# Four-layer attention kernel: the steps of layer A in another order (loads and statistics early, keys alternating with queries, G in halves, P read three tiles ahead)

## The chip, the cores and the metric

The kernel runs on one core of a Trainium2 chip. Five engines work side by side, each through a queue of its own in order: TensorE (PE: matrix products, which read SBUF and write PSUM; its weight loads, PEld, overlap the products), VectorE (DVE), ScalarE (ACT), GpSimd (POOL) and SyncE (SP, which here only issues DMAs). Semaphores make one engine wait for another. The metric is device time in microseconds (us) of the whole program; less is better.

## The reference

Four layers, A B A B, act on x of 2048 tokens by 640 values, each with 32 heads of 20 values and added to its own input. Layer A is linear attention over all tokens:

```
phi = lambda t: where(t > 0, t + 1, exp(t)) + 1e-6
pq, pk = phi(q), phi(k)                       # q, k, v = layernorm(x) @ wqkv
kv  = einsum("bhsd,bhse->bhde", pk, v)
z   = einsum("bhsd->bhd", pk)
num = einsum("bhqd,bhde->bhqe", pq, kv)
den = einsum("bhqd,bhd->bhq", pq, z)[..., None] + 1e-6
x   = x + reshape(num / den) @ wo
```

Layer B is softmax attention within four segments of 512 tokens, joined by a gate with a memory that earlier segments left. The change touches layer A alone.

## The kernel before, in words

**Numbers.** x is fp32. A matrix product takes each operand as a high and a low fp16 part and adds three products (high by high, high by low, low by high), so a product over 640 values, five blocks of 128, is 15 matmuls. Half a tile of tokens (128 tokens by 320 columns) is one such group of 15, in `proj_n` (L340 to 350); the text calls it a *unit*. A tile has two, a segment four tiles.

**Layer A in two passes.** All tokens' keys must be summed before any query can be answered. So the first pass (`a_first`, L451) makes, for each segment: normalized x (`norms`, L423: loads at L301, statistics at L304 to 316, normalized tile at L320), its transposes on PE (`turn`, L290), which ACT and DVE split into the two parts of `xT` (L294, L295), and `xs`, the normalized x split without transposing (L441, L442); then 8 units of keys (L458) and 8 of queries (L473), each followed by phi (`phi_a`, L355: ACT exp L359 and relu L361, POOL min and add L362, DVE addition L363). phi of keys, `pk`, is split by ACT (L464) and DVE (L465) and added to z (L470). phi of queries, P, is stored to DRAM by a DMA from POOL's queue (L476). Then `memory` (L479) multiplies keys with x itself, not with v: G = xsᵀ·pk, ten products of 12 matmuls (L489), five for the first half of the columns and five for the second, added to G by DVE (L496).

**The merge.** After the last segment's G, `merge` (L511) adds z over the partitions by PE (L526), copies it to `zb` (L527) and takes reciprocals (L528), scales G by them and splits it (L538 to L540), multiplies by the weight of v (L553: `kt`, evacuated by DVE and ACT at L558 to L565) and by the output weight (L583, L588: `wm`, L590, L591). `wm` then stands for k, v and the output at once. The last segment's query units are not needed for that and *fill* PE while ACT and DVE work on the steps of the merge.

**The second pass** (`a_second`, L628) reads P back tile by tile (`a_read`, L603: load on SP, POOL multiplies by zb at L608, DVE sums per head at L611 and L612, inverts, and multiplies at L614 into `pqi`), transposes it on PE and multiplies by `wm`. It reads two tiles ahead; `a_head` (L618) reads the first two and transposes the first. The second pass is woven with layer B's projections.

**What sets the order.** Only PE's order is the order in which the program is written; the tile scheduler orders DVE, ACT, POOL and SP by it with some freedom, each of them again in order once set. Steps are Python generators: `chain` runs them one after the other, `weave(main, aux, per)` takes `per` steps of the second after each of the first. The first layer A has nothing else to run beside it; its function `opening` (L951) weaves each segment's first pass with the preparation of seven weights (`w_prep`, L206: loads on SP, absolute maximum on DVE at L216 and L221, a transpose and a product on PE at L224 and L229 with DVE's L226 between, scales L232 to L235, splits by ACT L239 and DVE L240, and a store to DRAM on SP at L245) and with the next segment's `norms`. The second layer A runs beside layer B's attention in its first two segments and alone in the last two.

**Buffers.** Tiles tagged `row` (x, normalized x, pk, P) share ROWS = 10 buffers, phi's results share PQ = 5, and there are eight PSUM banks.

Of the kernel before, what the change touches and what calls it, by code (L numbers as in the profile page):

```python
# [21 lines left out]
P = 128  # L22
# [75 lines left out]
def weave(main, aux, per=1, drain=True):  # L98

    while True:  # L100
        try:
            r = next(main)
        except StopIteration as e:
            if drain:
                for r in aux:
                    yield r or 0.0
            return e.value
        yield r
        if not callable(r):
            for _ in range(per):  # L110
                x = next(aux, None)
                if x:
                    yield x


# [10 lines left out]
class Kernel:  # L126
# [295 lines left out]

    def norms(self, src, s, box, then=None):  # L423

        m = []
        for i in range(NT):
            m.append(self.moments(self.load_x(src, s, i)))
            if i == 0 and then:
                then()
        yield 0.0  # L430
        box.append(self.x_t())
        o = s % 2
        xs = self.sb.tile([P, C, 2, D], F16, tag="wo" if o else "w", name="xs", bufs=2 if o else 3)
        box.append(xs)
        nc = self.nc
        xh = self.normed(*m[0])
        yield 0.0
        for i in range(NT):
            nx = self.normed(*m[i + 1]) if i + 1 < NT else None
            yield from self.turn(xh, box[0], i)  # L440
# [10 lines left out]
    def a_first(self, s, box, w, L, behind=None):  # L451


        nc, sb = self.nc, self.sb
        xT, xs = box
        pk = []

        def keys():  # L458
            for i in range(NT):
                pk.append(sb.tile([P, 2, D], F16, tag="row", name="pk", bufs=ROWS))  # L460
                for n in range(2):
                    c = slice(n * HN, (n + 1) * HN)
                    e = self.phi_a(self.proj_n(xT, w("k"), i, n), self.inv["A", "k"])
                    nc.scalar.activation(pk[i][:, 0, c], e, AF.Copy, scale=self.k_scl)  # L464
                    nc.vector.scalar_tensor_tensor(pk[i][:, 1, c], e, self.k_scl, pk[i][:, 0, c],  # L465
                                                   op0=OP.mult, op1=OP.subtract)
                    if s == 0 and i == 0:
                        nc.vector.tensor_copy(L["z"][:, c], e)
                    else:
                        nc.vector.tensor_tensor(L["z"][:, c], L["z"][:, c], e, op=OP.add)  # L470
                    yield self.COST_N

# [25 lines left out]

        yield from keys()
        if s < NSEG - 1:  # L500
            for i in range(NT):
                yield from queries(i)
            if behind:
# [7 lines left out]
    def merge(self, L, wv, wo, fill):  # L511

# [31 lines left out]
        kt = []  # L544
        for t in range(C):
# [21 lines left out]
            yield 15 * (hi - lo) * COL  # L567
            if t % 2:
                yield from filled(1)
        wm = sb.tile([P, C, 2, D], F16, tag="wo", name="wm", bufs=2)  # L570
        yield from filled(1)
        for u in range(C):
            for n in range(2):
# [19 lines left out]
                yield 6 * HN * COL  # L593
            yield from filled(1)
        L["wm"] = wm
# [22 lines left out]
    def a_head(self, L, s, box):  # L618
# [5 lines left out]
        yield from self.a_read(L, s, 0, box["o"])  # L624
        yield from self.a_read(L, s, 1, box["o"])
        yield from self.turn(box["o"][0], box["oT"][0], 0)

    def a_second(self, src, dst, s, L, box, norm):  # L628
# [322 lines left out]
    def opening(self, src, stage, L, box):  # L951
# [13 lines left out]

        def w(n):
            if n != "v":
                for _ in a(n):
                    pass
            return self.w["A", n]  # L970

# [10 lines left out]
        k = a("k")  # L982
        n = self.norms(src, 0, cur, lambda: next(k))
        for _ in range(6):
# [7 lines left out]
        for s in range(NSEG):  # L992
            nxt = []
            if s == 0:
                aux = chain(a("q"), self.norms(src, 1, nxt), prep(("A", "v"), False))
            elif s == 1:
                aux = chain(prep(("A", "o"), False), self.norms(src, 2, nxt), late(), prep(("B", "v"), False))
            elif s == 2:
                aux = chain(self.norms(src, 3, nxt), prep(("B", "q"), False), prep(("B", "k"), False))
            else:  # L1000
                self.scales("A")
                self.w["A", "v"] = self.fetch(("A", "v"))
                aux = chain(prep(("B", "o"), False), last(), self.a_head(L, 0, box))
            yield from weave(self.a_first(s, cur, w, L), aux, per=2)
            cur = nxt

    def dense(self, layers, stage_ctx):
# [15 lines left out]
        while i < n:  # L1023
# [38 lines left out]
            else:  # L1062
                self.rate = R_MID
                for k in "kq":
                    wA[k] = self.fetch(("A", k))
                w = wA.__getitem__
                L = self.a_begin(i + 2)
                src = xs[i + 2]
                x0, x1, x2, x3 = [], [], [], []
                over = lambda st: lambda: st.get("attended")  # L1070
                yield from weave(fin, self.norms(src, 0, x0))
                yield from weave(self.a_first(0, x0, w, L, over(segs[2])),
                                 chain(when(segs[2], "attended", out[2]), self.norms(src, 1, x1)))
                yield from weave(self.a_first(1, x1, w, L, over(segs[3])),
                                 chain(when(segs[3], "attended", out[3]), self.norms(src, 2, x2)))
                yield from weave(self.a_first(2, x2, w, L), self.norms(src, 3, x3))
                wA["v"] = self.fetch(("A", "v"))
                yield from weave(self.a_first(3, x3, w, L), self.a_head(L, 0, box))
            i += 2
# [62 lines left out]
```

## Time and profile before

| | us |
|---|---|
| median of 3 runs (lowest, highest) | 1990.2 (1985.79, 1992.05) |
| the profiled execution | 1985.85 |
| its span in the trace | 1984.1 |
| PE busy | 1723.9 (87%) |
| DVE busy | 1298.5 (65%) |
| ACT busy | 963.8 (49%) |
| POOL busy | 636.7 (32%) |

The span runs from the first to the last recorded instruction; the profiled execution's own time has 1.75 us around it. Its mean granted TensorE clock is 0.959 of full speed. In the opening, 0 to 45 us hold the first normalized tiles and the preparation of the key weight; keys and queries of segments 0, 1 and 2 lie at 45 to 84 (keys of segment 0 begin earlier), 100 to 162 and 178 to 235 us, their G behind each for 16.3 us; keys of segment 3 at 251, its G at 268, its merge from 291 to 340. The second layer A's segment 2 begins at 1143 us, its last merge ends at 1292.

A row of the waits reads "PE ps L290 <- ACT xh L320: total us, times, longest": PE's instruction at L290, which writes `ps`, waited for ACT's instruction at L320, which writes `xh`. In a row of the timeline the numbers ahead are the start and the time in us, x5 counts the instructions, and the brackets at the end have the idle time before them and what ended it.

### The profile page before, as it was taken

What the parts mean: (1) busy time and instruction counts of PE and PEld (TensorE: products, weight loads), DVE (VectorE), ACT (ScalarE), POOL (GpSimd) and SP (SyncE); (2) the same over time, 40 slices, a digit from 0 to 9 for tenths busy, and PEclk for the clock granted to TensorE, in tenths of its full rate; (3) what the DMA queues carried; (4) which work ended last, traced back from release to release, by engine and by line L of the source; (5) the groups of instructions that cost most, each with busy time, mean ns of one, the idle gap of its engine ahead of it and who ended that gap; (6) DMA issues with size and microseconds to landing.
All of it is one profiled execution on the core that took longest, in us unless ns stands there. A gap on an engine that the chain in (4) does not pass through costs nothing.

```text
span 1984.1 us, 36713 instructions
## 1 busy us (share of the span) xinstructions
PE 1723.9 (87%) x13032; PEld 1056.0 (53%) x13032; DVE 1298.5 (65%) x4135; ACT 963.8 (49%) x1826; POOL 636.7 (32%) x1059
## 2 busy tenths in 40 slices
PE   4867887988898898999889989899889898898998
PEld 3545664655455456445545766565445544544555
DVE  7575656457677767767775454644767776767884
ACT  5453523334654554556555352323465466455553
POOL 3544535102222222324444453510221232222321
PEclk9887998999999999999999999899999999999999
DMA  5333334231222232323220312224123212323332
GB/s 192 131 129 117 126 133 164 90 129 48 71 94 65 88 108 80 103 93 114 68 91 14 107 34 100 107 89 147 56 71 99 94 58 95 105 61 95 127 101 87
DMA packets 107376, 192.55 MB, mean 97 GB/s; under 512 B 14124, under 2 KB 65452, under 8 KB 104504
## 3 DMA queue, kind: packets, MB, share of 16 engines
q1 hardware_dynamic: 93032, 137.44, 21.6%
q0 software_dynamic: 4944, 31.79, 4.4%
q10 hardware_dynamic: 9216, 20.98, 2.8%
q8 instruction: 103, 1.69, 0.4%
q14 instruction: 81, 0.66, 0.1%
HBM read 110.96 MB, written 78.64 MB: 96 GB/s over the span
## 4 chain that ended last, share of the span: by engine, by line
PE 58%; DVE 17%; POOL 9%; issue 8%; ACT 6%; DMA 2%; SPq 0%; POOLq 0%; ACTq 0%; DVEq 0%
PE ps L347 21%; PE ps L333 12%; PE ps L881 8%; DVE junk L824 6%; POOL e L362 5%; PE ps L489 4%; PE ps L854 3%; PE ps L290 3%; ACT pe L858 2%; PE ps L817 2%; PE ps L399 2%; PE ps L712 1%; DVE e L363 1%; POOL xs L442 1%; PE ps L894 1%
## 5 line engine op out<-in xcount | busy, mean ns | idle before, releaser
L824 DVE CUSTOM_DVE_ANT_0 junk<-ps,maskw 128x512 bf16<-128x512 f32 (+3 forms) x1024 | 498.9, 487 | 80.1 <-PE ps L817 27.3
L858 ACT ACTIVATE pe<-ps,lsc 128x512 f32<-128x512 f32 x640 | 394.2, 693 | 168.2 <-PE ps L854 142.2
L865 POOL TENSOR_SCALAR_AFFINE_SELECT pe<-pe 128x256 f32<-128x256 f32 (+1 forms) x640 | 236.7, 378 | 647.8 <-ACT pe L858 639.0
L347 PEld LDWEIGHTS <-xT 128*128 128x128 f16 x2880 | 287.8, 101 | 130.1 <-issue 17.5
L347 PEld LDWEIGHTS <-oT 128*128 128x128 f16 x1920 | 188.5, 99 | 88.0 <-issue 12.2
L362 POOL TENSOR_SCALAR e<-e 128x320 f32<-128x320 f32 x128 | 173.0, 1352 | 167.6 <-ACT e L359 163.1
L881 PE MATMUL ps<-pe,v 128*32 128x512 f32 (+3 forms) x2048 | 176.7, 477 | 11.9 <-POOL pe L865 4.6
L363 DVE TENSOR_TENSOR e<-e,r 128x320 f32<-128x320 f32 x128 | 64.5, 504 | 164.3 <-POOL e L362 163.3
L854 PE MATMUL ps<-qs,ks 62*128 62x384 f16 (+3 forms) x1024 | 130.3, 298 | 30.5 <-DVE mg L824 23.7
L347 PE MATMUL ps<-w_Aq,xT 128*128 128x320 f16 x960 | 147.7, 313 | 1.1 <-DVE mg L824 1.1
L347 PE MATMUL ps<-wm,oT 128*128 128x320 f16 x960 | 148.4, 309 | 0.0
L347 PE MATMUL ps<-w_Ak,xT 128*128 128x320 f16 x960 | 145.7, 311 | 1.3 <-DVE mg L824 0.7
L489 PE MATMUL ps<-pk,xs 128*128 128x320 f16 x960 | 138.3, 303 | 9.8 <-ACT pk L464 7.8
L347 PE MATMUL ps<-w_Bo,oT 128*128 128x320 f16 x960 | 141.2, 299 | 2.2 <-DVE mg L824 1.0
L333 PE MATMUL ps<-xT,w_Bq 128*128 128x512 f16 x600 | 140.3, 379 | 2.2 <-ACT r L372 1.2
L347 PE MATMUL ps<-w_Bv,xT 128*128 128x320 f16 x960 | 139.6, 299 | 2.5 <-DVE mg L824 2.5
L333 PE MATMUL ps<-xT,w_Bk 128*128 128x512 f16 x600 | 138.9, 380 | 0.6 <-DVE mg L824 0.6
L489 PEld LDWEIGHTS <-xs 128*128 128x128 f16 x960 | 94.7, 99 | 51.0 <-issue 13.9
L881 PEld LDWEIGHTS ps<-pe,v 128*32 128x32 f32 x2048 | 72.0, 117 | 89.5 <-issue 70.1
L817 PE MATMUL ps<-ks,qs 60*128 60x512 f16 (+3 forms) x1024 | 111.5, 298 | 8.7 <-DVE mg L824 4.4
L313 POOL TENSOR_TENSOR rs<-rs,mhalf 128x1 f32<-128x1 f32 x64 | 35.4, 553 | 238.2 <-DVE rs L312 237.3
L677 DVE SCALAR_TENSOR_TENSOR nat<-ps,nat 128x512 f16<-128x512 f32 x80 | 55.3, 691 | 85.6 <-ACT nat L676 82.4
(184 smaller groups left out, 2464.4 us busy)
## 6 DMA issues: line engine op xcount, KB each, us to landing
x<-xn ACTq DMA_DIRECT2D x48, 320.0 KB
qs<-qd SPq DMA_DIRECT2D x128, 120.0 KB
ks<-kd SPq DMA_DIRECT2D x128, 120.0 KB
xo<-x SPq DMA_DIRECT2D x48, 320.0 KB
pqd<-e POOLq DMA_DIRECT2D x64, 160.0 KB, 2.2
pqi<-pqd SPq DMA_DIRECT2D x32, 320.0 KB
qd<-nat SPq DMA_DIRECT2D x40, 256.0 KB
kd<-nat SPq DMA_DIRECT2D x40, 256.0 KB
```

The source lines that it names most:

```text
L290: nc.tensor.transpose(pt[:, (c - c0) * P:(c - c0 + 1) * P], src[:, c * P:(c + 1) * P], self.ident)
L333: nc.tensor.matmul(p, w[:, c, a, t * P:(t + 1) * P], xT[:, c, b, :], start=k == 0, stop=k == 3 * C - 1)
L347: nc.tensor.matmul(p, xT[:, c, a, i * P:(i + 1) * P], w[:, c, b, n * HN:(n + 1) * HN], start=k == 0, stop=k == 3 * C - 1)
L362: nc.gpsimd.tensor_scalar(e, e, 1.0, 1e-6, op0=OP.min, op1=OP.add)
L363: nc.vector.tensor_tensor(e, e, r, op=OP.add)
L489: nc.tensor.matmul(p, xs[:, i, a, c * P:(c + 1) * P], pk[i][:, b, n * HN:(n + 1) * HN], start=k == 0, stop=k == 3 * NT - 1)
L817: nc.tensor.matmul(bs[par][:, a:a + n], qs[r, p, i * P:(i + 1) * P], ks[r, p, :n], start=True, stop=True)
L824: nc.vector.tensor_tensor_reduce(junk[:, :n], bs[par][:, a:a + n], self.maskw[:, SEG - n:], 1.0, NEG, OP.add, OP.max, G["mg"][:, par, p, i ...
L854: nc.tensor.matmul(b[:, a:a + n], ks[r, p, j * P:(j + 1) * P], qs[r, p, j * P:], start=True, stop=True)
L858: nc.scalar.activation(e, b, AF.Exp, scale=self.lsc)
L865: nc.gpsimd.affine_select(d, d, pattern=pat, compare_op=OP.is_ge, fill=0.0, base=0, channel_multiplier=-1)
L881: nc.tensor.matmul(G["pv"][32 * h4:32 * h4 + 32, j * P:], v[j][:, h * E1:h * E1 + 32], G.pop((p, par, j)), start=j == 0, stop=j == 2, skip ...
```

## The change

`norms` is split: `moments_of` loads four tiles and takes their statistics, `norms` does the rest. In the opening, moments come ahead of a weight's preparation in each segment's auxiliary steps, and in segments 1 to 3 one auxiliary step is taken at a time instead of two. In the second layer A `norms` waits for eight more steps in the last but one segment (`pause`).

Keys and queries alternate, a tile of each in turn, if the query weight is there when the first pass of the segment starts. In the opening's first segment it isn't: there all keys go first, as before. The weight is there by the time the test is made again, and `queries(NT - 1)` is then issued once more: the last tile of queries is computed and stored twice, with the same values.

In the last segment two query tiles alternate with the keys, and two are left to fill. The z product comes ahead of G; G is made inside the merge, five products, then scaling and splitting of the first half beneath the other five; the two units of one query tile go in after the second `kt` tile, of the other two units one ahead of the products of `wm` and one behind them. `ones_column` comes later. `a_head` reads three tiles and waits for `wm`; `a_second` reads three ahead.

```diff
-    def norms(self, src, s, box, then=None):
+    def moments_of(self, src, s, box, then=None):
         m = []
         for i in range(NT):
             m.append(self.moments(self.load_x(src, s, i)))
             if i == 0 and then:
                 then()
+        box.append(m)
         yield 0.0
+    def norms(self, s, box):
+        nc, m = self.nc, box[0]
         box.append(self.x_t())
...
-        yield from keys()
-        if s < NSEG - 1:
+        if w("q", False) is None:
+            for i in range(NT):
+                yield from keys(i)
             for i in range(NT):
                 yield from queries(i)
+        else:
+            for i in range(NT - 1):
+                yield from keys(i)
+                if s < NSEG - 1 or i < 2:
+                    yield from queries(i)
+            yield from keys(NT - 1)
+        if s < NSEG - 1:
+            if w("q", False) is not None:
+                yield from queries(NT - 1)
             if behind:
                 yield behind
             yield from memory()
         else:
             wo = self.fetch_as(("A", "o"), ("A", "k"))
-            yield from memory()
-            yield from self.merge(L, w("v"), wo, chain(*(queries(i) for i in range(NT))))
+            yield from self.merge(L, w("v"), wo, memory(), chain(queries(2), queries(3)))
...
         L["zb"] = zb
         gs = []
         for n in range(2):
+            for _ in range(C):
+                yield next(memory)
             t = self.x_t()
             gs.append(t)
             for c in range(C):
...
-            yield from filled(2)
-        for v in L["v"]:
-            self.ones_column(v)
+        for _ in memory:
+            pass
...
-            if t % 2:
-                yield from filled(1)
+            if t == 1:
+                yield from filled(2)
+        for v in L["v"]:
+            self.ones_column(v)
         wm = sb.tile([P, C, 2, D], F16, tag="wo", name="wm", bufs=2)
         yield from filled(1)
         for u in range(C):
...
-            yield from filled(1)
         L["wm"] = wm
         yield from filled(8)
...
         yield from self.a_read(L, s, 0, box["o"])
         yield from self.a_read(L, s, 1, box["o"])
+        yield from self.a_read(L, s, 2, box["o"])
+        while L["wm"] is None:
+            yield 0.0
         yield from self.turn(box["o"][0], box["oT"][0], 0)
...
-            if i + 2 < NT:
-                yield from self.a_read(L, s, i + 2, o)
+            if i + 3 < NT:
+                yield from self.a_read(L, s, i + 3, o)
...
-                aux = chain(a("q"), self.norms(src, 1, nxt), prep(("A", "v"), False))
+                aux = chain(a("q"), self.moments_of(src, 1, nxt), prep(("A", "v"), False), self.norms(1, nxt))
             elif s == 1:
-                aux = chain(prep(("A", "o"), False), self.norms(src, 2, nxt), late(), prep(("B", "v"), False))
+                aux = chain(self.moments_of(src, 2, nxt), prep(("A", "o"), False), self.norms(2, nxt), late(),
+                            prep(("B", "v"), False))
             elif s == 2:
-                aux = chain(self.norms(src, 3, nxt), prep(("B", "q"), False), prep(("B", "k"), False))
+                aux = chain(self.moments_of(src, 3, nxt), prep(("B", "q"), False), self.norms(3, nxt),
+                            prep(("B", "k"), False))
...
-            yield from weave(self.a_first(s, cur, w, L), aux, per=2)
+            yield from weave(self.a_first(s, cur, w, L), aux, per=2 if s == 0 else 1)
...
-                yield from weave(self.a_first(2, x2, w, L), self.norms(src, 3, x3))
+                yield from weave(self.a_first(2, x[2], w, L), chain(moments(3), pause(8), norms(3)))
```

Where that moves instructions, shown at three places. On SP, the opening around the loads of segment 2's x (`in_A_x`; `stage` receives a weight, `wd_Ao` is the store of a prepared one). Before:

```order
L214 DMA stage<-in_B_wv 128x640 x5
L301 DMA x<-in_A_x 128x640
L245 DMA wd_Ao<-split 128x6400
L301 DMA x<-in_A_x 128x640 x3
L214 DMA stage<-in_B_wq 128x640 x5
```

The same place after:

```order
L219 DMA stage<-in_B_wv 128x640 x5
L306 DMA x<-in_A_x 128x640 x4
L250 DMA wd_Ao<-split 128x6400
L219 DMA stage<-in_B_wq 128x640 x5
L250 DMA wd_Bv<-split 128x6400
```

All four loads stand ahead of the store now; the next weight's loads and its store follow.

On PE, the product of z with a matrix of ones (`square`) in the first layer's last segment. Before:

```order
L489 LDWEIGHTS xs
L489 MATMUL ps<-pk,xs 128x320
L526 MATMUL ps<-z,square 128x320 x2
L347 LDWEIGHTS xT
L347 MATMUL ps<-w_Aq,xT 128x320
```

The same place after:

```order
L352 LDWEIGHTS xT
L352 MATMUL ps<-w_Ak,xT 128x320
L544 MATMUL ps<-z,square 128x320 x2
L497 LDWEIGHTS xs
L497 MATMUL ps<-pk,xs 128x320
```

It stood between G (L489) and the query units that fill; it stands between the last key unit (L352) and G (L497) now.

On POOL, the second segment of the opening, from its first steps of phi (`e`) to the first store of P (`pqd_1`); `rs` belongs to the statistics of the next x tiles, `xs` to their split. Before:

```order
L362 TENSOR_SCALAR e<-e 128x320 x7
L313 TENSOR_TENSOR rs<-rs,mhalf 128x1
L442 TENSOR_TENSOR xs<-xh,xs 128x640
L313 TENSOR_TENSOR rs<-rs,mhalf 128x1 x2
L442 TENSOR_TENSOR xs<-xh,xs 128x640
L313 TENSOR_TENSOR rs<-rs,mhalf 128x1
L362 TENSOR_SCALAR e<-e 128x320
L442 TENSOR_TENSOR xs<-xh,xs 128x640
L362 TENSOR_SCALAR e<-e 128x320
L476 DMA pqd_1_97<-e 128x320
```

The same place after:

```order
L367 TENSOR_SCALAR e<-e 128x320 x3
L318 TENSOR_TENSOR rs<-rs,mhalf 128x1 x2
L367 TENSOR_SCALAR e<-e 128x320
L318 TENSOR_TENSOR rs<-rs,mhalf 128x1
L484 DMA pqd_1_97<-e 128x320
L318 TENSOR_TENSOR rs<-rs,mhalf 128x1
L484 DMA pqd_1_97<-e 128x320
L367 TENSOR_SCALAR e<-e 128x320 x3
L484 DMA pqd_1_97<-e 128x320
```

The statistics stand some four steps of phi earlier, the splits `xs` behind them, and stores of P come among the keys' steps.

More of the change, by code (lines that the diff above doesn't have):

```diff
@@ L113, in weave, with pause @@
                     yield x
+def pause(n):
+    for _ in range(n):
+        yield 0.0
 def when(state, key, gen):
@@ L454, in a_first, with keys @@
         nc, sb = self.nc, self.sb
-        xT, xs = box
+        _, xT, xs = box
         pk = []
[L458 to L471, printed above, removed]
+        def keys(i):
+            pk.append(sb.tile([P, 2, D], F16, tag="row", name="pk", bufs=ROWS))
+            for n in range(2):
+                c = slice(n * HN, (n + 1) * HN)
+                e = self.phi_a(self.proj_n(xT, w("k"), i, n), self.inv["A", "k"])
+                nc.scalar.activation(pk[i][:, 0, c], e, AF.Copy, scale=self.k_scl)
+                nc.vector.scalar_tensor_tensor(pk[i][:, 1, c], e, self.k_scl, pk[i][:, 0, c],
+                                               op0=OP.mult, op1=OP.subtract)
+                if s == 0 and i == 0:
+                    nc.vector.tensor_copy(L["z"][:, c], e)
+                else:
+                    nc.vector.tensor_tensor(L["z"][:, c], L["z"][:, c], e, op=OP.add)
+                yield self.COST_N
         def queries(i):
@@ L964, in a, with w @@
             return preps[n]
-        def w(n):
-            if n != "v":
+        def w(n, now=True):
+            if now and n != "v":
                 for _ in a(n):
                     pass
-            return self.w["A", n]
+            return self.w.get(("A", n)) if now or ("A", n) in self.wd else None
         def late():
@@ L982, in opening @@
         k = a("k")
-        n = self.norms(src, 0, cur, lambda: next(k))
+        n = chain(self.moments_of(src, 0, cur, lambda: next(k)), self.norms(0, cur))
         for _ in range(6):
```

25 lines of the change are left out of this document (14 added, 11 removed).

## The prediction

> **What bounds the kernel now.** I read the shares first, then PE's waits in the stretches that the change touches, then a table of those stretches, then single rows. PE works for most of the span:
>
> ```profile
> PE 1723.9 (87%) x13032; PEld 1056.0 (53%) x13032; DVE 1298.5 (65%) x4135; ACT 963.8 (49%) x1826; POOL 636.7 (32%) x1059
> ```
>
> So a gain must come out of PE's idle time. The views of PE's waits say where that is: for 0 to 341 us (the first layer A up to its second pass), for 1140 to 1293 (the second layer A from segment 2 to its second pass), and, last line, for 341 to 930 (in 1293 to 1984 this row is the same). Columns: total us, times, longest us.
>
> ```profile
> PE ps L290 <- ACT xh L320: 42.9, 8, 11.3
> PE ps L229 <- DVE wm L226: 21.2, 6, 7.3
> PE ps L290 <- DVE rca L612: 8.7, 1, 8.7
> PE ps L224 <- DVE wm L221: 4.9, 1, 4.9
> PE ps L489 <- ACT pk L464: 3.1, 2, 2.6
> PE ps L588 <- ACT kt L564: 3.1, 1, 3.1
> ...
> PE ps L290 <- ACT xh L320: 8.3, 3, 5.7
> PE ps L290 <- DVE pqi L614: 5.3, 1, 5.3
> PE ps L489 <- ACT pk L464: 4.6, 1, 4.6
> PE ps L588 <- ACT kt L564: 3.1, 1, 3.1
> ...
> PE ps L290 <- DVE pqi L614: 7.4, 2, 4.1
> ```
>
> A transpose (L290) waits for a normalized tile or for a P tile, a weight's tiny product (L229) for its statistics. Each stands in PE's fixed order, so everything behind it stands too. The table by stage (stretch, length, busy PE, PEld, DVE, ACT, POOL, granted clock, DMA share, GB/s) has the keys and queries of segments 0, 1 and 2 of the opening, G of segment 3, its merge, the start of the second pass; then, of the second layer A, the keys and queries of segment 2, G of segment 3, its merge:
>
> ```profile
> 45.00:84.10 39.10, 25.14 (x159) 17.65 (x160) 26.63 (x65) 22.53 (x43) 23.21 (x22) 0.83 0.35 131
> 100.40:162.20 61.80, 40.39 (x268) 28.23 (x266) 42.29 (x94) 33.70 (x64) 31.15 (x29) 0.83 0.31 111
> 178.50:235.00 56.50, 42.61 (x269) 29.37 (x268) 28.95 (x75) 31.96 (x63) 30.17 (x27) 0.85 0.18 63
> 268.10:291.30 23.20, 18.64 (x123) 12.48 (x121) 12.69 (x24) 4.83 (x11) 4.90 (x5) 0.93 0.55 199
> 291.30:340.50 49.20, 36.75 (x299) 23.00 (x298) 32.12 (x67) 17.45 (x42) 27.13 (x30) 0.86 0.36 130
> 340.50:364.70 24.20, 20.90 (x146) 15.39 (x146) 14.42 (x37) 6.37 (x13) 4.34 (x6) 0.93 0.56 186
> 1142.90:1188.50 45.60, 37.30 (x262) 26.57 (x260) 26.68 (x60) 27.21 (x57) 26.88 (x24) 0.93 0.07 25
> 1221.10:1244.00 22.90, 18.10 (x123) 12.29 (x121) 9.53 (x20) 4.38 (x10) 4.43 (x4) 0.93 0.20 73
> 1244.00:1292.10 48.10, 39.09 (x300) 24.73 (x298) 31.30 (x68) 16.97 (x42) 27.45 (x30) 0.86 0.30 110
> ```
>
> Length less PE's busy time is idle time: 14.0 + 21.4 + 13.9 + 4.6 + 12.5 + 3.3 = 69.7 us in the first six stretches, 8.3 + 4.8 + 9.0 = 22.1 in the last three. Busy time is stretched too, since the clock is 0.83 to 0.93 there. Prices at full clock come from PE's timeline:
>
> ```profile
> 53.18 1.33 PE L290 MATMUL ps<-ident,xh 128*128 128x128 f32 x5 [8.23 <-ACT xh L320]
> 61.16 0.71 PE L290 MATMUL ps<-ident,xh 128*128 128x128 f32 x5
> 61.70 2.20 PE L347 MATMUL ps<-w_Aq,xT 128*128 128x320 f16 x15
> 84.09 16.46 PE L489 MATMUL ps<-pk,xs 128*128 128x320 f16 x120
> ```
>
> A matmul of 320 columns costs 16.46/120 = 137 ns, a unit of 15 (half a tile of keys or queries) 2.06, five transposes 61.70 − 61.16 = 0.54.
>
> **The change, part by part.** Line numbers are those of before.
>
> *Segment 1* of the opening now loads and measures segment 2's x tiles before any weight, and takes auxiliary steps one at a time, not two, so that more of them lie beside G. Before, three of the four loads stood on SP behind a store that waited for a weight's splits until 121.95, 21.5 us into the segment:
>
> ```profile
> 121.95 0.33 SPq L245 DMA_DIRECT2D wd_Ao<-split  x1
> 122.37 2.63 SPq L301 DMA_DIRECT2D x<-in_A_x  x3
> ```
>
> With that gone, what is late next is DVE. At full clock PE needs 16 units (33.0), 20 transposes (2.2) and 8 small matmuls (0.8); with 2.5 of waits and 1 for the clock that is 39.5 against 61.8, a gain of 22. But DVE was busy for 42.29 of those 61.8 us, and unless part of that slips into G it is the longer of the two: I take 20 (12 to 23).
>
> *Segment 2* gets its x tiles early, and segment 3's loads now stand behind another store, that of w_Bv. PE needs 33.0 + 2.2 + 0.9, 1.5 for the clock, and I add 7 for new waits: w_Bv's splits ahead of key work on ACT and DVE (2.7), the late loads (3), others (1.3). That is 44.6 against 56.5: 12 (9 to 16).
>
> *Segment 0* keeps keys before queries. Its long wait begins at 53.18 − 8.23 = 44.95, and I leave it there: w_Av's statistics now stand on PE ahead of the transposes, and DVE comes to them no earlier than
>
> ```profile
> 52.09 1.53 DVE L216 TENSOR_REDUCE wmx<-stage 128x1 f32<-128x640 f32 x2
> 53.66 0.16 DVE L221 TENSOR_REDUCE wm<-wmx 128x1 f32<-128x5 f32 x1
> ```
>
> By the second test of the weight it is ready, so the last tile of queries is issued twice: 30 matmuls, 4.1 us on PE, and two exponential steps and stores on POOL, hidden behind G. Of the idle 14.0 about 8 stays; the other 6, and about 1 of clock, go: 3 (0 to 5).
>
> *Keys and queries alternating.* POOL's steps for the exponentials followed each other by 76.14 − 73.35 = 2.79 for queries and 111.63 − 108.73 = 2.90 for keys, where PE needs 2.06:
>
> ```profile
> 73.35 1.27 POOL L362 TENSOR_SCALAR e<-e 128x320 f32<-128x320 f32 x1
> 75.45 0.61 POOL L476 DMA_DIRECT2D pqd<-e  x1 [0.82 <-DVE wm L226]
> 76.14 1.27 POOL L362 TENSOR_SCALAR e<-e 128x320 f32<-128x320 f32 x1
> 108.73 1.28 POOL L362 TENSOR_SCALAR e<-e 128x320 f32<-128x320 f32 x1 [4.20 <-ACT e L359]
> 111.63 1.28 POOL L362 TENSOR_SCALAR e<-e 128x320 f32<-128x320 f32 x1 [1.62 <-ACT e L359]
> ```
>
> A key's steps go from ACT to POOL, DVE and back to ACT, one after the other; a query's fill the gaps, and POOL's own work for one of each is 1.28 + 1.27 + 0.61 = 3.16, under PE's 4.12. So I let PE set the pace; that it doesn't is rival B.
>
> *Segment 3 and its merge* take, with keys of 8 × 2.06, 16.5 + 23.2 + 49.2 = 88.9. The merge's PE work less z (1.1, four short matmuls), 8 units and about 2 of slow clock is 36.75 − 1.1 − 16.5 − 2 = 17.2; with the four units that are left to fill it, 25.5. After: 12 units (24.7), 0.8 of small work, z 1.1, a wait, G 16.5, the 25.5, and 1.5 for the clock. The wait is new in size. G waits for the last pk now too, 4.6 in the second layer; but the z product, ahead of G now, waits for the last addition to z, and its copy, reciprocal and scaling of half 0 stand in DVE's queue ahead of the last key unit's own steps. By the group row the reciprocal is 2.12; the other two are put at 0.53 and 0.25, an estimate from the addition's row:
>
> ```profile
> L470 DVE TENSOR_TENSOR z<-z,e 128x320 f32<-128x320 f32 x30 | 15.8, 527 | 0.4
> L528 DVE RECIPROCAL rz<-zb 128x320 f32<-128x320 f32 x2 | 4.2, 2120 | 0.0
> ```
>
> 4.6 + 2.9 is 7.5; w_Bo's preparation shares ACT and DVE here, so I put it at 9 (5 to 12). The sum is 79.1, a gain of 10 (5 to 14). In exchange G's scaling for half 0 lies beneath half 1, P's first tiles are read further ahead (8.7 us of wait) and kt has two fill units behind it.
>
> *The second layer A.* Segment 2 has 33.0 + 2.2 and some 2 of waits left, 37 from 45.6: 8.5 (5 to 9); pause(8) puts its transposes behind their loads. Segment 3 with merge was 16.5 + 22.9 + 48.1 = 87.5; by the same terms, with 7 for the wait and 26 for the merge, 24.7 + 1.1 + 7 + 16.5 + 1 + 26 = 76.3: 11 (7 to 14). Segments 0 and 1 lie beside attention, which fills PE: 0 (−3 to 3).
>
> *P read three tiles ahead* in the second passes: the 7.4 us row, twice, is 14.8, and up to 2.4 of slow clock behind each. A third tile ahead adds two units of cover, 4.1 us, as long as the longest wait. Its row buffer is one of ten, and a wait for one could give some back: 15 (10 to 19.6).
>
> Sum: 20 + 12 + 3 + 10 + 8.5 + 11 + 15 = 79.5. The profiled execution took 1985.85, so 1906.35; the median of the runs shown is 1990.2, 4.35 more: 1910.7, rounded to 1911.
>
> One rule speaks against the alternation. The Trainium skill, page "SBUF — State Buffer", section "SBUF: two separate sides", says that a DVE instruction with two SBUF inputs and a GpSimd instruction that reads SBUF exclude each other, and that the one which starts second is blocked for the whole of the other. Alternation lays more of POOL's steps beside DVE's additions, so by this rule the sum would go the way of rival D. In the trace the mean z addition takes 527 ns (row above), and the longest is
>
> ```profile
> 1162.19 1.36 DVE L470 TENSOR_TENSOR z<-z,e 128x320 f32<-128x320 f32 x1
> ```
>
> so it bears the rule out for single instructions at most, and the sum keeps 0.53.
>
> **The rivals.**
>
> A, the forecast: 1911. Half the widths of the seven ranges and of ±3, taken as independent, make about ±12; its own range is 1896 to 1926. Chance 0.68.
>
> B, the chains set the pace of keys and queries though they alternate: 8 × 2.90 + 8 × 2.79 = 45.5 per segment against 33.0, 12.5 more in each of three (segments 1 and 2 here, segment 2 there), less some 2 that segment 1 already sets aside: 35.5 more, 1946. For it speaks DVE's 42.29 us in segment 1, against it that the two chains leave each other gaps on every engine. Chance 0.18.
>
> C, new waits at their low ends, each term at its high one: 23 + 16 + 5 + 14 + 9 + 14 + 19.6 + 3 = 103.6, so 1887. Chance 0.08.
>
> D, slower: POOL's steps hold each two-input DVE step of these stretches to 1.36, where it takes 0.53: 0.83 more. Three steps per key unit and one per query unit are 32 per segment, 26.6 us; with 28 in a last one, 23.2: 3 × 26.6 + 2 × 23.2 = 126 us. If more than 79.5/126 = 63% of that lies on PE's path, the gain is gone; at 80% it is 101, 21 slower, 2011. The mean of 527 ns speaks against it. Chance 0.04.
>
> E, the waits only move to the next instruction in PE's order: 1990, within 0.3% (6 us, about what a measurement of this kernel can tell from no change). For it: every stretch has several kinds of wait in a row. Chance 0.02.
>
> **How the numbers follow.** 1911 is A's. The range reaches from C's time to B's, 1887 to 1946: half of B, half of C, D and E, together 0.19, lie outside. Faster are A, B and C, 0.94; the same, E, 0.02; slower, D, 0.04.
>
> **What would show it.** In the changed profile, transposes of x should wait nowhere for more than 3 us in segments 1 and 2, but for 6 us or more near 45; the clock should be near 1 in those stretches; query matmuls with w_Aq should count 990; G of segment 3 should have 5 to 12 us of wait ahead of it; the second passes should have no 4 us wait for P. B would show as many waits of under a microsecond for PSUM banks or for pk, D as z additions with a mean above 0.8 us. Segments 1 and 2 at more than 50 us each, or new waits for row buffers in the second passes, would make the forecast wrong.

## The result and the profile after

The changed kernel takes 1916.9 us (median of 4 runs, 1911.5 to 1930.5) beside 1988.0 (4 runs, 1983.9 to 1992.1) for the kernel before: ratio 0.965, 95% interval 0.960 to 0.971. It is 71 us faster; 77 were forecast (1988 to 1911). The profiled execution took 1911.5 and is the fastest of the four; its gain on the profiled one of before is 74.4 us, and the terms below are measured against that.

PE's busy time fell by 20.7 us although it has 30 matmuls more, so part of the gain is clock (a mean of 0.959 of full speed before, 0.970 after); the rest of the 74 is idle time:

```profile
PE 1703.2 (89%) x13062; PEld 1048.7 (55%) x13062; DVE 1290.3 (68%) x4137; ACT 961.8 (50%) x1830; POOL 639.3 (33%) x1063
```

PE's waits in the changed kernel, first for 0 to 300 us, then for 1060 to 1230 (the second layer A's last segments). From 300 us to the end of the first merge at 312.6 PE shows no wait, so the first view stands against that of before for 0 to 341:

```profile
PE ps L295 <- ACT xh L325: 17.2, 4, 7.2
PE ps L544 <- ACT pk L472: 14.9, 2, 10.7
PE ps L295 <- DMA x<-in_A_x: 10.9, 1, 10.9
PE ps L229 <- DVE wm L226: 10.6, 2, 5.9
PE ps L234 <- DVE wm L231: 7.0, 4, 3.1
...
PE ps L544 <- ACT pk L472: 13.3, 2, 9.1
PE ps L295 <- ACT xh L325: 10.7, 2, 7.9
```

The waits for statistics (L229, L234) shrank from 26.1 to 17.6. Those for normalized tiles (L295 on `xh`) are smaller but not gone (11.3 of before's 42.9 us were the kernel's first wait, which has a row of its own here, for the load of x), and a new one stands at the z product (L544), which now precedes G: 14.9 and 13.3 us (the rows name ACT's pk, which ends beside the addition to z on DVE that the product reads). The places, from PE's timeline:

```profile
81.44 16.46 PE L497 MATMUL ps<-pk,xs 128*128 128x320 f16 x120
...
143.28 0.90 PE L295 MATMUL ps<-ident,xh 128*128 128x128 f32 x3 [7.16 <-ACT xh L325]
143.98 4.21 PE L352 MATMUL ps<-w_Aq,xT 128*128 128x320 f16 x15
...
201.39 0.90 PE L295 MATMUL ps<-ident,xh 128*128 128x128 f32 x3 [6.59 <-ACT xh L325]
...
264.86 1.40 PE L544 MATMUL ps<-z,square 128*128 128x320 f32 x2 [10.67 <-ACT pk L472]
270.47 1.41 PE L544 MATMUL ps<-z,square 128*128 128x320 f32 x2 [4.21 <-ACT pk L472]
271.67 17.95 PE L497 MATMUL ps<-pk,xs 128*128 128x320 f16 x120
...
1129.13 0.90 PE L295 MATMUL ps<-ident,xh 128*128 128x128 f32 x3 [7.88 <-ACT xh L325]
```

With the starts of each stretch in PE's timelines of both kernels, the gain lies elsewhere than forecast:

| stretch (its end) | before, us | after, us | gain | forecast |
|---|---|---|---|---|
| up to G of segment 0 | 84.1 | 81.4 | 2.7 | 3 |
| G of segment 0 | 16.3 | 16.3 | 0 | 0 |
| segment 1, with its G | 78.2 | 68.6 | 9.6 | 20 |
| segment 2, with its G | 72.7 | 62.7 | 10.0 | 12 |
| segment 3 and merge, to the first P transpose after it | 89.2 | 83.6 | 5.6 | 10 |
| second passes and layer B, and the second layer A's segments 0 and 1 | 802.4 | 786.0 | 16.4 | 7.5 |
| second layer A, segment 2 with G | 61.9 | 66.6 | −4.7 | 8.5 |
| its segment 3 and merge | 87.3 | 82.0 | 5.2 | 11 |
| the last second pass and layer B | 692.0 | 662.5 | 29.5 | 7.5 |

The first passes where layer A runs alone gave 28 us, not the 64.5 forecast for these six terms; the rest gave 46, not 15.

### The profile page after: what moved, and what is told of

It is laid out like the page before. It is cut to its first block, busy times and chain, and to the rows that moved or that the text cites. A ratio compares the mean times of both kernels' runs of the same rounds, so it can differ in the third digit from the quotient of the medians.

```text
span 1909.8 us, 36713 instructions
## 1 busy us (share of the span) xinstructions
PE 1703.2 (89%) x13062; PEld 1048.7 (55%) x13062; DVE 1290.3 (68%) x4137; ACT 961.8 (50%) x1830; POOL 639.3 (33%) x1063
## 4 chain that ended last, share of the span: by engine, by line
PE 35%; DVE 6%; ACT 3%; POOL 3%; issue 3%; POOLq 0%; ACTq 0%; DVEq 0%
PE ps L352 13%; PE ps L338 6%; PE ps L904 4%; PE ps L497 4%; DVE junk L847 3%; POOL e L367 2%; PE ps L877 2%; PE ps L295 2%; ACT pe L881 1%; PE ps L840 1%; PE ps L735 1%; PE ps L404 1%; PE ps L917 1%; DVE nat L700 1%; ACT nat L699 0%
## 5 line engine op out<-in xcount | busy, mean ns | idle before, releaser
L352 PEld LDWEIGHTS <-xT 128*128 128x128 f16 x2910 | 288.9, 100 | 129.7 <-issue 17.6
L352 PEld LDWEIGHTS <-oT 128*128 128x128 f16 x1920 | 185.4, 98 | 87.5 <-issue 11.8
L904 PE MATMUL ps<-pe,v 128*32 128x512 f32 (+3 forms) x2048 | 169.3, 459 | 15.2 <-ACT pe L881 5.9
L352 PE MATMUL ps<-w_Aq,xT 128*128 128x320 f16 x990 | 151.7, 312 | 2.6 <-DVE xT L300 1.5
L352 PE MATMUL ps<-wm,oT 128*128 128x320 f16 x960 | 142.9, 301 | 2.2 <-ACT oT L299 1.4
L352 PE MATMUL ps<-w_Ak,xT 128*128 128x320 f16 x960 | 143.5, 307 | 1.3 <-DVE mg L847 0.7
L352 PE MATMUL ps<-w_Bo,oT 128*128 128x320 f16 x960 | 141.2, 299 | 2.2 <-DVE mg L847 1.0
L352 PE MATMUL ps<-w_Bv,xT 128*128 128x320 f16 x960 | 139.6, 299 | 1.9 <-DVE mg L847 1.9
L497 PE MATMUL ps<-pk,xs 128*128 128x320 f16 x960 | 139.8, 304 | 0.5 <-DVE mg L847 0.5
L904 PEld LDWEIGHTS ps<-pe,v 128*32 128x32 f32 x2048 | 69.7, 114 | 90.9 <-issue 68.6
L497 PEld LDWEIGHTS <-xs 128*128 128x128 f16 x960 | 95.2, 100 | 40.7 <-issue 4.2
```

The lines of the kernel that those rows point to most:

```text
L352: nc.tensor.matmul(p, xT[:, c, a, i * P:(i + 1) * P], w[:, c, b, n * HN:(n + 1) * HN], start=k == 0, stop=k == 3 * C - 1)
L497: nc.tensor.matmul(p, xs[:, i, a, c * P:(c + 1) * P], pk[i][:, b, n * HN:(n + 1) * HN], start=k == 0, stop=k == 3 * NT - 1)
L904: nc.tensor.matmul(G["pv"][32 * h4:32 * h4 + 32, j * P:], v[j][:, h * E1:h * E1 + 32], G.pop((p, par, j)), start=j == 0, stop=j == 2, skip ...
```

## The experiments

Two accounts stood against each other. The forecast's: PE sets the pace in the changed first passes, and reading P further ahead saves PE's waits for P, 15 us. The *pace theory*, from the table above: phi's chain over ACT, POOL and DVE still sets it, and the reading ahead is worth three times as much. Medians in us, ratios to the kernel before on the same chip:

| kernel | median | ratio, 95% interval |
|---|---|---|
| before (of the result) | 1988.0 | 1 |
| changed | 1916.9 | 0.965 (0.960 to 0.971) |
| e_read3: P three ahead alone | 1940.2 | 0.973 (0.970 to 0.977) |
| e_step: P's load and POOL's product ahead alone | 1947.7 | 0.979 (0.976 to 0.981) |
| e_early: e_read3 and the early loads | 1910.8 | 0.961 (0.959 to 0.962) |
| e_noalt: changed, keys before queries | 1915.8 | 0.963 (0.960 to 0.965) |
| e_zlate: changed, z within G | 1925.6 | 0.968 (0.965 to 0.972) |
| e_nodup: changed, no second issue | 1906.2 | 0.958 (0.956 to 0.960) |
| e_stores_sp: changed, P stored by SP | 1884.0 | 0.947 (0.945 to 0.949) |
| e_dvephi: changed, POOL's step left out | 1837.2 | 0.923 (0.920 to 0.926) |
| e_dve2: e_nodup, that step on DVE | 1846.0 | 0.929 (0.926 to 0.932) |
| e_dve2_early: e_early, that step on DVE | 1844.8 | 0.928 (0.925 to 0.931) |

**e_read3.** In the kernel before:

```diff
         yield from self.a_read(L, s, 1, box["o"])
+        yield from self.a_read(L, s, 2, box["o"])
+        while L["wm"] is None:
+            yield 0.0
...
-            if i + 2 < NT:
-                yield from self.a_read(L, s, i + 2, o)
+            if i + 3 < NT:
+                yield from self.a_read(L, s, i + 3, o)
```

Expected: 

> The kernel before with one part of the change alone: P is read three tiles ahead in the second passes. By the forecast's account this part is worth 15 us, about 1973 beside a kernel before at 1988. By the pace theory (the first passes, where layer A runs alone, are held by phi's chain over ACT, POOL and DVE, so that the changed kernel gained only 28 us before 313 us and 0.5 in the second layer's last two segments, and the second passes with the layers B behind them gave the other 46) it is worth 35 to 46, 1942 to 1953, with the two waits for P gone and the clock of the last stretch nearer to 1.00 than to 0.98. If that last stretch was only a lucky clock in one profiled run, the gain is 15 to 25.

Measured: 1940.2, 50 us less, just past the upper end of the pace theory. Of before's waits those for P are gone, and so is much of another kind. First before, then e_read3; each view is PE's waits from 300 us to 1900, where `m` is a row maximum that layer B's attention sends to PE:

```profile
PE pm L837 <- DVE m L834: 46.7, 23, 3.6
```

```profile
PE pm L840 <- DVE m L837: 29.0, 19, 2.8
```

Why a read of P should delay a row maximum shows on DVE in the kernel before, around PE's wait of 2.79 us at 469.86:

```profile
463.26 0.82 DVE L611 TENSOR_REDUCE rca<-pqi 128x32 f32<-128x640 f32 x1 [0.93 <-POOL pqi L608]
464.00 0.41 DVE L824 CUSTOM_DVE_ANT_0 junk<-ps,maskw 128x256 bf16<-128x256 f32 x1
...
465.14 0.82 DVE L611 TENSOR_REDUCE rca<-pqi 128x32 f32<-128x640 f32 x1
...
467.44 0.82 DVE L614 TENSOR_TENSOR pqi<-pqi,rca 128x640 f32<-128x640 f32 x1
...
469.63 0.17 DVE L834 SCALAR_TENSOR_TENSOR m<-mg,m 128x16 f16<-128x16 f32 x1
```

Two tiles of P are worked on at once, in among the maxima (L824, L834): DVE waits for POOL's product at L611, and the sums and products of P stand ahead of `m`.

**e_step.** P's load and POOL's product were put into a function of their own, `a_load`, called one tile earlier than the rest of `a_read`:

```diff
+            if i + 3 < NT:
+                self.a_load(L, s, i + 3, box["ld"])
             if i + 2 < NT:
-                yield from self.a_read(L, s, i + 2, o)
+                yield from self.a_read(L, s, i + 2, o, box["ld"])
```

Expected: 

> The kernel before with only P's load and POOL's multiplication three tiles ahead, while DVE's sums, reciprocals and multiplications stay two ahead. If the read-ahead alone (50 us less) gained more than PE's waits for P because DVE had stood at POOL's product, 16 us in 12 places, with attention's row maxima behind it, half of the 50 or more comes already here: 1950 to 1965, and PE's waits for the row maxima fall from 47 us to about 30. If only the place of DVE's own steps counts, PE's waits for P and for the maxima stay, and it takes 1980 or more.

Measured: 1947.7, 42 of the 50 us; more than was expected. PE's waits for `m` came to 28.2, and DVE's waits for POOL's product, here of before and of e_step, 345 to 1900 us, fell to a third (in e_read3 to 8.3):

```profile
DVE rca L611 <- POOL pqi L608: 16.0, 12, 2.5
```

```profile
DVE rca L617 <- POOL pqi L608: 5.2, 5, 2.4
```

So most of the read-ahead's worth is that P's load and product are done when DVE comes to them, not that DVE's own steps are written earlier. Whether those steps, which the scheduler places, also moved in this kernel was not separated. Nor is all of either gain read-ahead: both kernels also hold the first P transposes back until `wm` is there, and in the merges of before PE waits 8.7 and 5.3 us at these. In the profiles 10.9 of e_read3's 38.9 us and 12.5 of e_step's 44.5 come before a layer's second pass starts (in the first layer A, and in the second one's segments 2 and 3); the other 28 and 32 come elsewhere.

**e_early.** e_read3 with `moments_of`, the new auxiliary chains and `per=2 if s == 0 else 1`, as in the change; keys, queries and merge as before.

Expected: 

> The kernel before with two parts of the change: P read three tiles ahead, and the early loads and statistics with the auxiliary steps one at a time. Keys and queries don't alternate, and the merge is the old one. The changed kernel gained 12 us in the opening's segments 1 and 2 over the kernel with the read-ahead alone. If the early loads made that, this one takes 1916 to 1926, and the segments' G begins as early as in the changed kernel; if alternation was needed for it, it stays near 1940.

Measured: 1910.8, 29 us below e_read3 and 6 below the changed kernel. In the profiles the first P transpose after the merge starts at 310.5 us, in e_read3 at 335.8. The early loads account for the rest of the change's gain; nothing of it needed the alternation or the new merge, which are worth at most the 5 us by which e_nodup (below) is faster than e_early.

**e_noalt.** In the changed kernel, for all segments but a layer's last:

```diff
+        elif s < NSEG - 1:
+            for i in range(NT):
+                yield from keys(i)
+            for i in range(NT - 1):
+                yield from queries(i)
```

Expected: 

> The changed kernel with all keys ahead of all queries again, in every segment but a layer's last. By the forecast's account alternation is what lets PE set the pace: without it 12 us more in each of three segments, about 37 in all, 1954. By the pace theory the chain's pace is 2.8 to 2.9 us a unit in either order: within 8 us of the changed kernel.

Measured: 1915.8 beside 1916.9: no difference. The order of keys and queries doesn't matter here; the 37 us of the forecast's account are not there.

**e_zlate.** In the changed kernel's merge, five of G's products ahead of z:

```diff
         rz = self.row("rz")
+        for _ in range(C):
+            yield next(memory)
         for n in range(2):
...
-            for _ in range(C):
+            for _ in range(C if n else 0):
                 yield next(memory)
```

Expected: 

> The changed kernel with the z product moved behind G's first five products. The 4.2 us wait between the two z matmuls goes in both layers, and 1 to 2 us of what is queued ahead of the last keys' steps: 8 to 14 us less by either account of the chain; the wait of about 10 us for the last keys stays, ahead of G instead of ahead of z, if phi's chain is what is late, and shrinks to 5 if the copies and reciprocals of z made it.

Measured: 1925.6, no gain; by the medians 9 us worse, with intervals that overlap. A miss for both accounts. In its PE timeline G now waits for the last keys (L497), and behind it kt, in small pieces, for G's scaling (L574):

```profile
258.58 0.42 PE L497 MATMUL ps<-pk,xs 128*128 128x320 f16 x1 [4.03 <-ACT pk L472]
...
264.38 0.42 PE L497 MATMUL ps<-pk,xs 128*128 128x320 f16 x1 [4.52 <-ACT pk L472]
265.72 9.38 PE L497 MATMUL ps<-pk,xs 128*128 128x320 f16 x50 [0.91 <-DVE pk L473]
...
293.35 0.20 PE L574 MATMUL ps<-xT,w_Av 128*128 128x80 f16 x1 [1.20 <-ACT xT L561]
```

G runs undisturbed 6 us earlier than in the changed kernel (from 265.7, there 271.7), but kt waits 4.5 us in all, and the second pass begins at 317.9, not 314.2: what was won ahead of G was given back behind it. In both kernels PE stands for the last keys; moving z only changed which instruction stands.

**e_nodup.** `w("q", False)` is tested once, ahead of the first keys, and its answer kept.

Expected: 

> The changed kernel without the second issue of segment 0's last query tile: 30 matmuls, 4.1 us of PE time less. If PE sets the pace there, G of segment 0 begins 4 us earlier and the median falls by 4, less than the runs scatter; if phi's chain does, 4 to 6.

Measured: 1906.2. In the profiles G of segment 0 begins at 76.9 instead of 81.4, 4.6 us earlier, and the second pass at 309.8 instead of 314.2, 4.4 earlier. The medians differ by 10.8; the changed kernel's own runs scatter over 19 us, so the second issue is put at the 4.4 that the profiles show.

**e_stores_sp.** `QUEUES` with `'sync'` in place of the first `'gpsimd'`.

Expected: 

> The changed kernel with P stored from SP's queue instead of POOL's. By the pace theory each store holds POOL for 0.8 us of waiting for DVE's addition and 0.6 of its own; 32 query units lie where layer A runs alone, 46 us at most, and with key chains beside them I expect a third to two thirds of it, 15 to 30 us less than the changed kernel. By the forecast's account PE sets the pace: no difference beyond 5 us, or slower where a store on SP holds loads behind it.

Measured: 1884.0, 33 us below the changed kernel, a little more than the 15 to 30 expected. In the profiles the first P transpose comes at 294.4 us instead of 312.6, and segments 2 and 3 of the second layer A take 137.1 instead of 148.7, so the gain lies in the first passes. This is POOL in the changed kernel in segment 1, ahead of PE's wait at 143.28, where `e` is phi and L484 the store of P:

```profile
132.98 1.28 POOL L367 TENSOR_SCALAR e<-e 128x320 f32<-128x320 f32 x1 [1.62 <-ACT e L364]
135.08 0.61 POOL L484 DMA_DIRECT2D pqd<-e  x1 [0.82 <-DVE e L368]
135.72 1.41 POOL L451 TENSOR_TENSOR xs<-xh,xs 128x640 f16<-128x640 f32 x1
137.22 1.27 POOL L367 TENSOR_SCALAR e<-e 128x320 f32<-128x320 f32 x1
139.32 0.62 POOL L484 DMA_DIRECT2D pqd<-e  x1 [0.82 <-DVE e L368]
140.02 1.28 POOL L367 TENSOR_SCALAR e<-e 128x320 f32<-128x320 f32 x1
```

After each query's step POOL waits 0.82 us for DVE's addition, because the store stands next in its queue, and the next unit's step, whose input is ready, stands behind that. ACT is held by the same chain:

```profile
135.48 0.52 ACT L299 ACTIVATE xT<-ps 128x384 f16<-128x384 f32 x1
141.86 0.56 ACT L472 ACTIVATE pk<-e,k_scl 128x320 f16<-128x320 f32 x1 [5.86 <-DVE e L368]
142.32 0.91 ACT L325 ACTIVATE xh<-x,nb,rs 128x640 f32<-128x640 f32 x1
```

ACT stands for 5.86 us at a key's pk, with the normalized tile for which PE waits right behind it. The tile's statistics were ready; it was late because of the keys. Whether the wait in POOL's queue or the 0.61 us of the store itself costs more was not separated.

**e_dvephi.** Leaves out the addition of 0.000001 in phi; POOL has no step in it:

```diff
-        nc.gpsimd.tensor_scalar(e, e, 1.0, 1e-6, op0=OP.min, op1=OP.add)
-        nc.vector.tensor_tensor(e, e, r, op=OP.add)
+        nc.vector.scalar_tensor_tensor(e, e, 1.0, r, op0=OP.min, op1=OP.add)
```

Expected: 

> The changed kernel with phi's minimum and addition in one DVE step, and POOL's step left out (with it the addition of 0.000001 to phi is left out). By the pace theory POOL is the longest link of the chain: without its 1.28 us the unit's pace falls below PE's 2.06, PE's 7 us waits for normalized tiles and the 10.7 us ahead of the z product shrink to 3 or less, and 40 to 55 us go, 1862 to 1877; more than the 33 of the stores on SP. If the other waits of the first passes (weights' statistics, x's loads) are what is left, it gives no more than SP's stores did: 1884 or above.

Measured: 1837.2, 80 us below the changed kernel, more than expected. Its second pass begins at 275.1 instead of 314.2 (39 us), and 38 more go from the start of that pass's last segment to the start of the second layer's second pass (501.4 instead of 539.8 us). PE's waits for 0 to 300 us:

```profile
PE ps L229 <- DVE wm L226: 7.4, 2, 4.2
PE ps L295 <- ACT xh L325: 6.2, 3, 3.0
PE ps L234 <- DVE wm L231: 3.3, 3, 1.6
PE ps L543 <- DVE z L477: 3.0, 1, 3.0
PE ps L543 <- ACT pk L471: 0.7, 1, 0.7
```

The waits for tiles, for statistics (both rows) and for z all shrink: 17.2, 17.6 and 14.9 became 6.2, 10.7 and 3.7. The first layer's second passes are as long as in the changed kernel (83.0, 143.7, 165.9 beside 82.7, 145.6, 166.6 for three segments), so nothing was gained there.

**e_dve2 and e_dve2_early.** The whole computation, with `nc.vector.tensor_scalar` in place of `nc.gpsimd.tensor_scalar` at that line, in e_nodup and in e_early.

Expected of e_dve2: 

> The changed kernel, the last query tile issued once, with POOL's step of phi (minimum and addition) put on DVE ahead of DVE's own addition: nothing is left out. Leaving POOL's step out gave 1837. The step costs DVE some 0.4 us for 128 units, mostly beside PE work: if POOL was the link that set the pace, most of the gain stays, 1835 to 1860; if DVE now sets it, 1870 or more.

Expected of e_dve2_early: 

> The same step on DVE in the kernel with the read-ahead and the early loads alone: keys before queries, the old merge. With POOL in the chain, alternation and the new merge were worth nothing or less than nothing (1911 without them, 1906 with them and one issue of each tile). If they are worth nothing in themselves, this one is within 8 us of its partner; if they gain once PE can set the pace, as the prediction had it, the partner is 15 to 35 us faster.

Measured: 1846.0 and 1844.8, 71 to 72 us less than the changed kernel, and 142 to 143 less than before; of that the step itself, against e_nodup and e_early, is 60 and 66. The step takes 0.41 us on DVE, by the group row for 40 to 250 us of e_dve2, where POOL takes 1.39 (the changed kernel, 45 to 265):

```profile
L367 DVE TENSOR_SCALAR e<-e 128x320 f32<-128x320 f32 x56 | 22.9, 411 | 1.9 <-ACT e L364 1.9
```

```profile
L367 POOL TENSOR_SCALAR e<-e 128x320 f32<-128x320 f32 x56 | 78.0, 1393 | 54.4 <-ACT e L364 51.6
```

With POOL out of the chain, alternation and the new merge are still worth nothing: the two kernels differ by 1.2 us.

## Why the prediction was right, and where it was not

The time was right, near the forecast's middle, but as a sum of errors of both signs: 36 us too much for the first passes, 31 too little for the rest. That they nearly cancel is luck.

Of the signs that the prediction named, the 990 query matmuls came, the second passes have no 4 us wait for P, and the z additions got no longer. Most others failed: transposes in segments 1 and 2 wait up to 7.16 and 6.59 us, not 3; the clock there is 0.87 and 0.92, not near 1; the wait ahead of G is 14.9 and 13.3 us, not 5 to 12; and segment 1 took 50.7 us, where more than 50 for both segments was to make the forecast wrong (segment 2 took 44.8).

*Read ahead, right in kind, the size two to three times too small.* The prediction counted PE's waits for P, 14.8 us, and 2.4 of clock behind each. Those waits are gone, as it said. It left out that P's steps share DVE's queue with attention's row maxima: in the second passes of segments 0 to 2 of both layers PE's waits for `m` fell from 29.0 to 17.8 us in the changed kernel, beside the 14.7 for P, while these six stretches became 36 us shorter; the other 11 are PE's busy time, which the same work stretched before. The last stretch ran at 0.98 of full clock before and 1.00 after, so its 29.5 us hold some 12 (2% of 618 us of PE work) of clock. Part of that may be a lucky run, since the profiled run was the fastest of four, but not much: in the other kernels that read P whole three tiles ahead (all but e_step) this stretch takes 663.9 to 670.3 us, so at least 21.7 of the 29.5 us stay. And e_read3, alone, has 50 us in its medians, 10.9 of its profile's 38.9 in the first passes and merges, as said above.

*"So I let PE set the pace": wrong.* The prediction compared POOL's work for a key and a query (3.16) with PE's (4.12). What counts is not POOL's work alone but how long the chain is and what stands in its queues: between two steps POOL waits for DVE's addition because of the store, and ACT waits at pk for the same addition. In segment 3 of the changed kernel POOL's steps still follow each other by 2.8 to 2.9 us or more:

```profile
247.19 1.91 POOL L367 TENSOR_SCALAR e<-e 128x320 f32<-128x320 f32 x1 [2.34 <-ACT e L364]
...
253.80 1.27 POOL L367 TENSOR_SCALAR e<-e 128x320 f32<-128x320 f32 x1
256.60 1.27 POOL L367 TENSOR_SCALAR e<-e 128x320 f32<-128x320 f32 x1
259.49 1.28 POOL L367 TENSOR_SCALAR e<-e 128x320 f32<-128x320 f32 x1 [1.62 <-ACT e L364]
262.38 1.28 POOL L367 TENSOR_SCALAR e<-e 128x320 f32<-128x320 f32 x1 [1.62 <-ACT e L364]
265.30 1.96 POOL L367 TENSOR_SCALAR e<-e 128x320 f32<-128x320 f32 x1 [0.96 <-ACT e L364]
```

So rival B's mechanism holds for the first passes; e_stores_sp and e_dvephi show it, e_noalt that alternation changes nothing, and the forecast's 64.5 us for the first passes became 28. Its sign, many short waits, did not come (they are few and long), and its size fits only in part: the three segments that it names fell short by 25.6 us, not 35.5, and the two merges by 10.2 more. That rival's own time, 1946, missed since the read-ahead gave 30 us more than it assumed.

*Segment 1*, 20 forecast and 9.6 measured: the waits for loads went, as said, and e_early shows that the early loads made the gain (with its G the segment takes 69.4 us there, 68.6 in the changed kernel, 78.2 before); the chain's 7.16 us wait took their place. DVE, which the prediction took for the next limit, was not: the row of this stretch for the changed kernel, then the same stretch in e_dvephi (columns as in the table of before), has it busy for 57% and for 78%.

```profile
97.70:148.40 50.70, 38.92 (x255) 26.79 (x254) 29.14 (x69) 26.50 (x53) 28.65 (x27) 0.87 0.23 85
```

```profile
91.70:128.10 36.40, 34.49 (x255) 24.89 (x253) 28.27 (x68) 24.11 (x49) 7.14 (x11) 1.00 0.33 118
```

*Segment 3 and merge*, 10 and 11 forecast, 5.6 and 5.2 measured: the new wait was put at 9 (5 to 12) and 7, and is 14.9 and 13.3. Of the 4.21 between the two z products 3.0 is the copy, reciprocal and scaling on DVE, near the 2.9 forecast; the other 10.7 is the chain's backlog. And the new order of the merge earned little of what was gained: e_read3, with the old merge, has 2.6 and 6.2 us of gain in these two stretches.

*Second layer A, segment 2*, 8.5 forecast, −4.7 measured. 7.88 and 2.77 us waits for tiles replaced 5.67 and two short ones; the same backlog, since the stretch takes 66.6 us here and 51.1 in e_dvephi. It is the only stretch that became slower, and the only one where alternation shows: without it (e_noalt) the stretch takes 63.6.

*Segments 0 and 2* came out at 2.7 and 10.0, near the forecast (3 and 12). In segment 0 the terms hold too: 8.5 us of wait are left where 8 were forecast, and the second issue costs the 4.4 us that the prediction priced at 4.1. In segment 2 the number was met by another wait: 44.8 us without G, where 44.6 were forecast with 7 set aside for splits and late loads. With the same loads and splits, e_dvephi takes 37.4 there, so most of the 7 were the chain's, and that the number was met is luck.

*Rival D*, DVE held by POOL, is refuted as a mechanism of the mean: z additions (DVE, 45 to 260 us) took 531 ns before and 507 after. For single instructions the rows show a block. The z addition of 1.36 us in the prediction (1162.19, before) ended at 1163.55, 0.34 after the POOL instruction beside it:

```profile
1161.50 1.71 POOL L442 TENSOR_TENSOR xs<-xh,xs 128x640 f16<-128x640 f32 x1
```

The Trainium skill's page "SBUF — State Buffer", section "SBUF: two separate sides", states a full block of the one that starts second; these rows agree. Rivals C and E fell with the measured time; C came nearest on the read-ahead only.

## What to carry to other kernels

A chain that hops over engines is timed by its length and by what stands behind each hop in an in-order queue, not by the busy share of any engine: look for a store or a conversion that waits in the queue of the engine that the next unit needs. Before reordering the work of the waiting engine, try the cheaper edits, a store on another queue (33 us here) or a step on another engine (60 to 66), since they also show what an order can still earn (here the order of keys and queries earned nothing, that of the loads 29 us). And when a load is read further ahead, count the steps of other streams that stood behind its consumers, not only the waits of PE for it.

## What was not expected of the hardware

In the changed kernel POOL's step takes 1.28 us alone and up to 1.96 in places: the two rows at 247.19 and 265.30 above are 1.91 and 1.96 us. Beside them stand these DVE instructions, a split of a weight and one of pk:

```profile
247.07 0.88 DVE L245 SCALAR_TENSOR_TENSOR split<-stage,scl_Bo,split 128x640 f16<-128x640 f32 x1
...
265.70 0.42 DVE L473 SCALAR_TENSOR_TENSOR pk<-e,k_scl,pk 128x320 f16<-128x320 f32 x1
```

POOL's two steps end 1.15 and 1.14 us after them (249.10 and 247.95; 267.26 and 266.12). Five more steps that start beside such a split, at 66.06, 123.47, 126.73, 171.29 and 232.36, end 1.14 to 1.15 us after it too, so the extra time is read as waiting for DVE's instruction to end; no run varied it. A wait of 7 us costs PE more than itself: the 15 matmuls behind the one at 143.28 take 4.21 us (row above), where they take 2.20 in undisturbed stretches. And POOL needs 1.39 us in the mean for a minimum and an addition on 128 by 320 values for which DVE needs 0.41.
